# Seven weight clamps on VectorE instead of GpSimd, and the fifth tile's first products issued in the startup, in a fused attention and two-mixer kernel

## The chip, the cores and the metric

One core of one Trainium2 chip. The metric is the device time of one execution in microseconds; the median of three runs of the kernel before is 668.87 us (668.62 to 670.48).

## What is computed

Three stages follow each other on a batch of 4 sequences of 768 tokens; all numbers are float32.

```python
# 1. linear attention with a per-channel decay, 8 heads of 48
cur = einsum('bhd,bhe->bhde', u * kt, vt)
y[:, :, t] = einsum('bhd,bhde->bhe', rt, state + cur)
state = w * state + einsum('bhd,bhe->bhde', kt, vt)
# 2. a gated mixer, 384 -> 1024 -> 384
h = relu(x @ w_in)
conv_out = sum_k conv_w[k] * shifted(h, k)      # 3 taps over the tokens
x1 = (h * sigmoid(conv_out)) @ w_out
# 3. a normalised mixer, 384 -> 1536 -> 384
xn = (x1 - mean) / sqrt(var + 1e-6) * g_ln
out = x1 + relu(xn @ w_ch1) @ w_ch2
```

## The kernel before, in words

**Attention** works on 24 tiles of 128 tokens (n = 0 to 23), six to a sequence. `attn_tile(n)` is a generator. Its first part multiplies the tile's r and k by tables of decay powers (line 373, one VectorE instruction over both). Tiles 0 to 5 then take `light_tile`: z = r times k on VectorE (line 322), then at the next step dot products on TensorE, copies on ScalarE, a triangular select and a product on GpSimd (`affine_select`, line 335), then the products that make the output, and its split into a high and a low part. `decayed_k(n)` (line 252) multiplies the keys by their table. `startup()` (line 434) writes out by hand the order of tiles 0 to 3 and mixes in the first steps of the weight work. `attention()` (line 461) is a generator over the later tiles, from n = EARLY = 4 on; each `next` of it is one step.

**Weights** arrive in 22 pieces as pairs of 32-bit words (64-bit floats) and are converted on the chip. `wjob` (line 141) makes for each piece a load on SP's queue and a generator `steps()`: ScalarE takes the absolute value, `magnitude` (line 121) clamps it in place (line 125), VectorE shifts it and joins two more bit fields (`decode`, line 128), ScalarE writes the high part, and VectorE the low part (lines 168 and 170). `ahead()` (line 152) makes absolute value and clamp of the next piece at once after the last bit operation of a piece. The engine of the clamp is chosen there by the number of the piece, `me`: VectorE for pieces 0 to 9 (the first mixer's weights), GpSimd for pieces 10 to 21 (the second mixer's). `wdo(count)` (line 210) advances this work by so many steps. Pieces 15 to 21 are the second half of w_ch1 and the last four pieces of w_ch2.

**The first mixer** (`mixer1`, line 600) takes eight blocks of 384 tokens, and for each block eight rows of 128 channels: nine matmuls up, then ReLU on ScalarE, the convolution's centre tap on ScalarE (line 533) and its two other taps on VectorE (line 535), sigmoid, gate and a split into high and low part, and nine matmuls down, two or three rows later. After each row, `after1` (line 834) is called twice; it takes an attention step whenever `pace` has reached 5 (2.5 a call in the first two blocks, 2 later), and weight steps. In the first block that is `wdo(2)` at each call; from the second on one step at every fifth call.

**The second mixer** (`mixer2`, line 616) takes six blocks of 512 tokens with twelve rows of channels each. `after2` (line 860) advances the weight work by three steps after each row, until all pieces are made, which is within the first block. Between the blocks the next 512 tokens are fetched and normalised.

**Order.** Calls through `vo`, `ao`, `go`, `so` and `pe` keep the order of the program among themselves on their engine (VectorE, ScalarE, GpSimd, SP's queue, TensorE). All of TensorE's matmuls, the weight work and the early tiles are written this way. The other VectorE, ScalarE and GpSimd instructions (of the mixers, and most of the later tiles') are placed between them by a scheduler that simulates the program when it is built. Instructions made through these wrappers all show line 76 in the profile; the tile's name tells them apart: `wdec` is a weight piece in work, `rk` a tile's r and k, `kks` its decayed keys, `z` the product, `wih`, `wil`, `woh`, `wol`, `c1h`, `c1l`, `c2h`, `c2l` the high and low parts of the four weight matrices.

Of the kernel before, what the change touches and what calls it, by code (L numbers as in the profile page):

```python
# [49 lines left out]
def body(ctx, tc, r, k, v, w, u, w_in, conv_w, w_out, g_ln, w_ch1, w_ch2, rkT, krv, small, out):  # L50
# [28 lines left out]
    vo = InOrder(nc.vector)  # L79
    ao = InOrder(nc.scalar)  # L80
    so = InOrder(nc.sync)
    go = InOrder(nc.gpsimd)
# [35 lines left out]
    def words(st, n):  # L118
        return [st[:, 0:2 * n].rearrange("p (n two) -> p n two", two=2)[:, :, i] for i in range(2)]

    def magnitude(st, n, engine=go):

        t = ap.tile([128, WN], F32, tag="wd", name="wdec", bufs=2)[:, 0:n]
        ao.activation(out=t, in_=words(st, n)[1].bitcast(F32), func=AF.Abs)
        engine.tensor_scalar(out=t, in0=t, scalar1=W_MIN, scalar2=W_MAX, op0=ALU.max, op1=ALU.min)
        return t

    def decode(st, n, t):

        lo, hi = words(st, n)  # L130
        ti = t.bitcast(I32)
        vo.tensor_scalar(out=ti, in0=ti, scalar1=5, scalar2=2, op0=ALU.logical_shift_left,
                         op1=ALU.logical_shift_right)
        yield
        vo.scalar_tensor_tensor(out=ti, in0=lo, scalar=29, in1=ti, op0=ALU.logical_shift_right, op1=ALU.bitwise_or)
        yield
        vo.scalar_tensor_tensor(out=ti, in0=hi, scalar=-(2 ** 30), in1=ti, op0=ALU.bitwise_and, op1=ALU.bitwise_or)
# [3 lines left out]
    def wjob(src, n, hi, lo, scale=None):  # L141

        st, mag = [], []

        def load():
            st.append(io.tile([128, 2 * WN], I32, tag="st" if me >= 4 else "first", name="st", bufs=3 if me >= 4 else 4))
            dst = st[0][:, 0:2 * n]
            if len(src.shape) == 3:
                dst = dst.rearrange("p (a n) -> p a n", a=src.shape[1])
            so.dma_start(out=dst, in_=src.bitcast(I32))  # L150

        def ahead():
            if not mag:
                mag.append(magnitude(st[0], n, vo if me < 10 else go))

        def steps():
            ahead()
            t = mag[0]
            yield from decode(st[0], n, t)
            if me + 1 < min(len(wjobs), w_loaded[0]):  # L160
                wjobs[me + 1][2]()
            if len(src.shape) == 3:
                t = t.rearrange("p (a n) -> p a n", a=src.shape[1])
            kw = {} if scale is None else {"scale": gl[:, scale:scale + 1]}
            ao.activation(out=hi, in_=t, func=AF.Copy, **kw)
            yield
            if scale is None:
                vo.tensor_tensor(out=lo, in0=t, in1=hi.bitcast(F32), op=ALU.subtract)
            else:
                vo.scalar_tensor_tensor(out=lo, in0=t, scalar=kw["scale"], in1=hi.bitcast(F32),  # L170
                                        op0=ALU.mult, op1=ALU.subtract)
        me = len(wjobs)
        wjobs.append((load, steps(), ahead))
        return len(wjobs) - 1

# [28 lines left out]
    def wload(count):  # L204

        while w_loaded[0] < min(count, len(wjobs)):
            wjobs[w_loaded[0]][0]()
            w_loaded[0] += 1

    def wdo(count=1, last=None):  # L210

        for _ in range(count):
            while w_done[0] < (len(wjobs) if last is None else last + 1):
                wload(w_done[0] + 3)
                if next(wjobs[w_done[0]][1], "end") != "end":
                    break
                w_done[0] += 1
# [8 lines left out]
    def load_tile(n):  # L226
        if n >= NT:
            return
        own = "e" if n < EARLY else ""
        rk = io.tile([PR, 2, NP, C], F32, tag="rk" + own, name="rk", bufs=EARLY if own else 3)  # L230
        kt = io.tile([128, DM], F32, tag="k" + own, name="kt", bufs=EARLY if own else 2)
        rv = io.tile([128, DM + H * 64], F32, tag="rv" + own, name="rv", bufs=EARLY if own else 3)
        s_ = so
        s_.dma_start(out=rk.rearrange("x a p c -> x (a p c)"), in_=rkT[n])
        s_.dma_start(out=kt, in_=krv[n, :, 0:DM])
        if n >= EARLY:
            load_rows(n, s_, rv)
        loaded[n] = (rk, kt.rearrange("x (h d) -> x h d", h=H), rv[:, 0:DM].rearrange("x (h d) -> x h d", h=H),
                     rv[:, DM:].rearrange("x (h d) -> x h d", h=H), rv)
# [12 lines left out]
    def decayed_k(n):  # L252

        if n < LIGHT:
            vo.tensor_tensor(out=kks[:, n % 2, 0, :, 0:D], in0=loaded[n][1], in1=tku[:, 0], op=ALU.mult)
            return
        inputs(n).tensor_tensor(out=kks[:, n % 2, :, :, 0:D], in0=loaded[n][1].unsqueeze(1).to_broadcast([128, 2, H, D]), in1=tku,
                         op=ALU.mult)
# [45 lines left out]
    def inputs(n):  # L304
        return vo if n < HAND else nc.vector
# [102 lines left out]
    def state_sum(n):  # L408
        vt = loaded[n][3]
        if n % TPB != TPB - 1:  # L410
            pst = sums[n] = ps_a.tile([128, NP, D], F32, tag="pa", name="pst")
            for h in range(H):
                q0 = 64 * (h % 2)
                pe.matmul(pst[q0:q0 + 64, h // 2, :], lhsT=kks[:, n % 2, 0, h, :], rhs=vt[:, h, 0:D], start=True,
                          stop=True)

    def state_update(n):
        first, last = n % TPB == 0, n % TPB == TPB - 1
        v_, a_, g_ = ordered(n)
        if not last:  # L420
            pst = sums.pop(n)
            sn = ap.tile([PR, NP, D], F32, tag="sn", name="sn")
            if first:
                a_.activation(out=sn, in_=pst[0:PR], func=AF.Copy)
            else:
                v_.tensor_tensor(out=sn, in0=pst[0:PR], in1=state[0], op=ALU.add)
            if n % TPB < TPB - 2:
                state[0] = ap.tile([PR, NP, D], F32, tag="sw", name="sw")
                v_.tensor_tensor(out=state[0], in0=sn, in1=w128.to_broadcast([PR, NP, D]), op=ALU.mult)
            sb = sbd[(n + 1) % 2]  # L430
            a_.activation(out=sb[0:D, :, 0:D], in_=sn[0:D], func=AF.Copy)
            a_.activation(out=sb[64:PR, :, D:2 * D], in_=sn[64:PR], func=AF.Copy)

    def startup():

        tiles = {n: attn_tile(n) for n in range(EARLY + 1)}

        def on(n):
            next(tiles[n], None)

        decayed = decayed_k
        on(0), decayed(0), on(0)
        on(1), state_sum(0), state_update(0), decayed(1), on(1), state_sum(1)
        wdo(1)
        on(0), on(2), state_update(1), decayed(2)
        wdo(2)
        on(2), state_sum(2), on(0)
        wdo(1)
        on(1), on(3), state_update(2), decayed(3)
        wdo(2)  # L450
        on(3), state_sum(3), on(1)
        wdo(2)
        on(2), state_update(3)
        wdo(3)
        on(2), on(3)
        wdo(1)
        on(3)
        wdo(4)
        return tiles

    def attention(tiles):

        def go_on(n):
            if 0 <= n < NT:
                next(tiles.setdefault(n, attn_tile(n)), None)

        n = EARLY
        go_on(n)
        decayed_k(n)
        yield  # L470
        load_tile(n + 2)
        decayed_k(n + 1)
        go_on(n)
        yield
        for n in range(EARLY, NT):
            state_sum(n)
            state_update(n)
            go_on(n - 1)
            go_on(n + 1)
            yield  # L480
            go_on(n)
            go_on(n + 1)
            yield
# [333 lines left out]

    cst = tables()
    feed = attention(startup())
    for _ in conv_weights(cst):  # L820
        pass
# [120 lines left out]
```

## Time and profile before

| | us |
|---|---|
| median of three runs | 668.87 |
| the profiled execution | 670.22 |
| its span, first to last instruction | 668.4 |
| TensorE busy (matmuls) | 633.3 |
| VectorE busy | 437.4 |
| ScalarE busy | 261.9 |
| GpSimd busy | 122.5 |

Times in the trace are counted from the span's first instruction, in microseconds. A row of a timeline gives the start, the duration, the engine, the line, the operation, the tile written and the tiles read, the shape, and how many equal instructions in a row were merged; in brackets stands how long the engine had been idle before, and what ended that, as inferred from semaphores. PE is TensorE, DVE is VectorE, ACT is ScalarE, POOL is GpSimd and SPq is the queue on which SyncE issues loads and stores. Matmuls overlap, so TensorE's busy time counts only where it leaves gaps. The granted clock (PEclk) is a share of full speed.

### The profile page before, as it was taken

To read this page: it belongs to the slowest core of one execution; us is meant where nothing else is said; L and a number is where in the kernel's file an instruction comes from. 1 tells how busy PE (TensorE), PEld (TensorE's weight loads), DVE (VectorE), ACT (ScalarE), POOL (GpSimd) and SP (SyncE) were. 2 spreads that over 40 slices of the span, in tenths; PEclk is the share of its full clock that TensorE was granted. 3 is DMA by queue.
4 is the path that set the end of the run, shared out by engine and by line. 5 is a ranking of instruction groups with operands and counts; after the bars stand their busy time and mean duration, and the time that the engine had idled before them with its cause. 6 is when DMAs were issued, how large, how long until landed. Compare 5 with 4: busy or idle time off the path is not lost.

```text
span 668.4 us, 11712 instructions
## 1 busy us (share of the span) xinstructions
PE 633.3 (95%) x4803; PEld 573.2 (86%) x4803; DVE 437.4 (65%) x793; ACT 261.9 (39%) x514; POOL 122.5 (18%) x126
## 2 busy tenths in 40 slices
PE   9948898999998898999999999999999999999996
PEld 5747888989987897899998789999999899999995
DVE  7979999999999999878777953413422422422211
ACT  3455555465655655566764421211221111221110
POOL 6301621330332214112003620100100100100000
PEclk9876898999999999999999999999999999999999
DMA  8916434435262533102205302002001100200101
GB/s 268 313 49 209 144 106 151 135 100 185 71 215 68 173 114 115 37 1 84 71 13 177 95 0 89 8 0 86 10 0 48 49 0 29 67 0 7 42 0 52
DMA packets 25295, 56.51 MB, mean 85 GB/s; under 512 B 2961, under 2 KB 15378, under 8 KB 25234
## 3 DMA queue, kind: packets, MB, share of 16 engines
q1 hardware_dynamic: 25234, 55.68, 26.2%
q8 instruction: 40, 0.66, 0.4%
q14 instruction: 21, 0.17, 0.1%
HBM read 46.24 MB, written 9.44 MB: 83 GB/s over the span
## 4 chain that ended last, share of the span: by engine, by line
PE 50%; DVE 36%; ACT 4%; issue 4%; DMA 3%; POOL 1%; SPq 0%; DVEq 0%; ACTq 0%
PE acc L76 24%; PE psm L76 24%; DVE c L535 8%; DVE wdec L76 6%; DVE aT L389 3%; DVE c L516 3%; DVE gl L522 3%; DVE rk L373 2%; DMA x1b<-x_dram 1%; DVE rk L76 1%; DVE a L380 1%; DVE xl L398 1%; PE pxt L76 1%; DVE av L378 1%; DMA rk<-in_rkT_dram 1%
## 5 line engine op out<-in xcount | busy, mean ns | idle before, releaser
L549 DVE SCALAR_TENSOR_TENSOR rl<-psm,rh 128x512 fp32r<-128x512 f32 x72 | 49.6, 689 | 135.1 <-ACT rh L548 131.6
L548 ACT ACTIVATE rh<-psm 128x512 fp32r<-128x512 f32 x72 | 43.0, 597 | 196.1 <-PE psm L76 195.9
L76 PE MATMUL acc<-c2l,rh 128*128 128x384 f32 x288 | 97.2, 338 | 0.4 <-DVE c2l L76 0.4
L76 PE MATMUL acc<-c2h,rh 128*128 128x384 f32 x288 | 97.1, 337 | 0.0
L76 PE MATMUL acc<-c2h,rl 128*128 128x384 f32 x288 | 97.1, 337 | 0.0
L535 DVE SCALAR_TENSOR_TENSOR c<-h,tables,c 128x384 f32<-128x384 f32 x128 | 89.9, 704 | 7.0 <-ACT c L533 6.4
L76 PE MATMUL psm<-xnh,c1h 128*128 128x512 f32 x216 | 87.2, 404 | 0.8 <-ACT c1h L76 0.8
L76 PE MATMUL psm<-xnh,c1l 128*128 128x512 f32 x216 | 85.3, 395 | 0.3 <-DVE c1l L76 0.3
L76 PE MATMUL psm<-xnl,c1h 128*128 128x512 f32 x216 | 85.5, 396 | 0.0
L76 PE MATMUL psm<-xh,wih 128*128 128x386 f32 x192 | 71.3, 371 | 13.4 <-DVE xl L76 4.4
L76 PE MATMUL psm<-xl,wih 128*128 128x386 f32 x192 | 67.7, 353 | 0.0
L76 PE MATMUL psm<-xh,wil 128*128 128x386 f32 x192 | 67.7, 352 | 0.0
L76 PE MATMUL acc<-woh,gh 128*128 128x384 f32 x192 | 66.5, 347 | 0.0
L76 PE MATMUL acc<-woh,gl 128*128 128x384 f32 x192 | 65.0, 339 | 0.1
L76 PE MATMUL acc<-wol,gh 128*128 128x384 f32 x192 | 65.0, 339 | 0.0
L76 PEld LDWEIGHTS acc<-c2l,rh 128*128 128x128 f32 x288 | 54.1, 188 | 3.6 <-DVE c2l L76 0.8
L76 PEld LDWEIGHTS acc<-c2h,rh 128*128 128x128 f32 x288 | 54.1, 188 | 3.2
L76 POOL TENSOR_SCALAR wdec<-wdec 128x768 f32<-128x768 f32 (+1 forms) x13 | 40.1, 3085 | 86.4 <-ACT wdec L76 86.4
L76 PEld LDWEIGHTS acc<-c2h,rl 128*128 128x128 f32 x288 | 54.1, 188 | 0.0
L572 POOL TENSOR_TENSOR rs<-rs,nhalf 128x1 f32<-128x1 f32 x24 | 16.4, 691 | 199.4 <-DVE rs L571 198.9
L76 PEld LDWEIGHTS psm<-xh,wih 128*128 128x128 f32 x192 | 38.1, 199 | 17.0 <-ACT woh L76 4.6
L521 ACT ACTIVATE gh<-c 128x384 fp32r<-128x384 f32 x64 | 33.5, 523 | 47.2 <-DVE c L516 46.7
(133 smaller groups left out, 1142.3 us busy)
## 6 DMA issues: line engine op xcount, KB each, us to landing
rk<-in_rkT_dram SPq DMA_DIRECT2D x24, 448.0 KB, 4.4
st<-in_moe_w_ch_dram SPq DMA_DIRECT2D x12, 768.0 KB, 6.0
rv<-in_krv_dram SPq DMA_DIRECT2D x18, 448.0 KB, 4.8
kt<-in_krv_dram SPq DMA_DIRECT2D x24, 192.0 KB, 4.3
x_dram<-x SPq DMA_DIRECT2D x24, 192.0 KB, 2.1
x1b<-x_dram SPq DMA_DIRECT2D x24, 192.0 KB, 3.1
out_dram<-x1b SPq DMA_DIRECT2D x24, 192.0 KB, 1.9
st<-in_moe_w_in_dram SPq DMA_DIRECT2D x6, 512.0 KB, 9.2
```

What stands on the lines that cost most here:

```text
L76: return lambda *args, **kw: tc.keep_in_program_order(op(*args, **kw))
L373: inputs(n).tensor_tensor(out=rk, in0=rk, in1=trk, op=ALU.mult)
L378: v_.tensor_tensor(out=av, in0=kks[:, n % 2, 1, :, 0:D], in1=rt, op=ALU.mult)
L380: v_.tensor_reduce(out=a8.rearrange("x (q p) o -> x q (p o)", q=2), in_=av.rearrange("x (p q) d -> x q p d", q=2), axis=AX.X, op=ALU.add)
L389: v_.copy_predicated(out=aT[:, q], mask=later.bitcast(I32).unsqueeze(1).to_broadcast([128, NP, C]), data=dps[q])
L516: v_.tensor_tensor(out=st["c"], in0=st["h"][:, 1:T + 1], in1=st["c"], op=ALU.mult)
L521: a_.activation(out=st["gh"], in_=st["c"], func=AF.Copy)
L522: v_.tensor_tensor(out=st["gl"], in0=st["c"], in1=st["gh"].bitcast(F32), op=ALU.subtract)
L535: v_.scalar_tensor_tensor(out=c, in0=h[:, o:o + T], scalar=cw[:, tap, f:f + 1], in1=c, op0=ALU.mult, op1=ALU.add)
L548: a_.activation(out=gh[:, 0:cols], in_=ps[:, 0:cols], func=AF.Relu)
L549: v_.scalar_tensor_tensor(out=gl_[:, 0:cols], in0=ps[:, 0:cols], scalar=0.0, in1=gh[:, 0:cols].bitcast(F32), op0=ALU.max, op1=ALU.subtract)
L572: g_.tensor_tensor(out=rs[:, 1:2], in0=rs[:, 0:1], in1=nhalf, op=ALU.pow)
```

## The change

The clamp's engine becomes VectorE for pieces 15 to 21 as well, so GpSimd keeps those of pieces 10 to 14 (and the small one of the convolution's weights). In `startup()` the last four weight steps are split: after the first of them stand the first step of tile 4 (its r and k products and z) and its keys. In `attention()` the same two calls and the first `yield` are taken out.

```diff
--- before.py
+++ after.py
@@ -151,7 +151,7 @@
 
         def ahead():
             if not mag:
-                mag.append(magnitude(st[0], n, vo if me < 10 else go))
+                mag.append(magnitude(st[0], n, vo if me < 10 or me >= 15 else go))
 
         def steps():
             ahead()
@@ -455,7 +455,9 @@
         on(2), on(3)
         wdo(1)
         on(3)
-        wdo(4)
+        wdo(1)
+        on(4), decayed(4)
+        wdo(3)
         return tiles
 
     def attention(tiles):
@@ -465,9 +467,6 @@
                 next(tiles.setdefault(n, attn_tile(n)), None)
 
         n = EARLY
-        go_on(n)
-        decayed_k(n)
-        yield
         load_tile(n + 2)
         decayed_k(n + 1)
         go_on(n)
```

## Rows read from the trace of the kernel before

**Rows 1.** The page's chain that ended last: shares of the span by engine.

```profile
PE 50%; DVE 36%; ACT 4%; issue 4%; DMA 3%; POOL 1%; SPq 0%; DVEq 0%; ACTq 0%
```

**Rows 2.** Busy time by stage: stage and length, engines (instructions), PEclk, DMA share, GB/s.

```profile
52.50:60.00 7.50, 7.49 (x45) 6.84 (x45) 7.46 (x12) 3.40 (x7) 3.05 (x3) 0.50 0.43 138
52.50:130.00 77.50, 72.11 (x752) 66.08 (x753) 77.40 (x122) 42.09 (x85) 27.43 (x18) 0.90 0.50 156
130.00:280.00 150.00, 142.56 (x1550) 130.81 (x1549) 145.92 (x239) 84.04 (x176) 39.32 (x34) 1.00 0.38 122
346.00:396.00 50.00, 48.51 (x243) 42.51 (x242) 40.55 (x70) 21.35 (x34) 21.89 (x10) 1.00 0.29 91
396.00:655.00 259.00, 259.00 (x1318) 233.85 (x1317) 76.62 (x161) 44.35 (x77) 9.50 (x16) 1.00 0.09 28
```

**Rows 3.** Timeline of TensorE: start us, us, instruction [idle before <-releaser].

```profile
52.51 2.08 PE L76 MATMUL dps<-rk 48*128 48x128 f32 x16 [7.16 <-ACT wih L76]
```

**Rows 4.** Timeline of VectorE, 40 to 55 us.

```profile
40.99 1.42 DVE L76 SCALAR_TENSOR_TENSOR wdec<-st,wdec 128x512 int32<-128x512 int32 x2
...
44.01 0.69 DVE L76 TENSOR_TENSOR wil<-wdec,wih 128x512 fp32r<-128x512 f32 x1 [1.26 <-ACT wih L76]
...
46.88 1.27 DVE L535 SCALAR_TENSOR_TENSOR c<-h,tables,c 128x384 f32<-128x384 f32 x2 [0.68 <-ACT c L533]
...
51.19 1.22 DVE L76 TENSOR_TENSOR rk<-rk,tables 112x1024 f32<-112x1024 f32 x1
...
53.32 0.69 DVE L76 TENSOR_TENSOR z<-rk 112x512 f32<-112x512 f32 x1
53.92 0.55 DVE L76 TENSOR_TENSOR kks<-kt,tables 128x384 f32<-128x384 f32 x1
```

**Rows 5.** Timeline of ScalarE, 40 to 60 us.

```profile
42.97 0.49 ACT L532 ACTIVATE h<-psm 128x386 f32<-128x386 f32 x1 [1.63 <-PE psm L76]
43.35 0.62 ACT L76 ACTIVATE wih<-wdec 128x512 fp32r<-128x512 f32 x1
```

**Rows 6.** Timeline of SP's DMA queue.

```profile
42.47 15.17 SPq L76 DMA_DIRECT2D st<-in_moe_w_out_dram  x3
```

**Rows 7.** Timeline of GpSimd.

```profile
56.65 1.96 POOL L335 TENSOR_SCALAR_AFFINE_SELECT aT<-aT 128x512 f32<-128x512 f32 x2 [11.31 <-ACT aT L334]
...
294.07 3.29 POOL L76 TENSOR_SCALAR wdec<-wdec 128x768 f32<-128x768 f32 x1 [16.71 <-ACT wdec L76]
...
379.85 3.41 POOL L76 TENSOR_SCALAR wdec<-wdec 128x768 f32<-128x768 f32 x1 [2.81 <-ACT wdec L76]
```

**Rows 8.** The list of waits, 85 to 290 us: us in total, times, longest.

```profile
DVE c L535 <- ACT c L533: 1.5, 2, 1.0
```

**Rows 9.** Timeline of VectorE: a clamp of the startup, then 362 to 392 us.

```profile
34.66 0.56 DVE L76 TENSOR_SCALAR wdec<-wdec 128x768 f32<-128x768 f32 x1 [1.26 <-ACT wdec L76]
...
362.27 0.56 DVE L569 BATCH_NORM_STATS2 bs<-x1b 128x6 f32<-128x384 f32 x1 [3.85 <-DMA x1b<-x_dram]
...
368.71 1.10 DVE L76 SCALAR_TENSOR_TENSOR wdec<-st,wdec 128x768 int32<-128x768 int32 x1
...
372.19 1.02 DVE L76 SCALAR_TENSOR_TENSOR c1l<-wdec,smallt,c1h 128x768 fp32r<-128x768 f32 x1 [0.40 <-ACT c1h L76]
...
374.60 2.29 DVE L76 SCALAR_TENSOR_TENSOR wdec<-st,wdec 128x768 int32<-128x768 int32 x2
...
381.13 0.98 DVE L76 SCALAR_TENSOR_TENSOR wdec<-st,wdec 128x768 int32<-128x768 int32 x1
...
384.97 2.44 DVE L76 SCALAR_TENSOR_TENSOR wdec<-st,wdec 128x768 int32<-128x768 int32 x2
...
390.33 1.95 DVE L76 SCALAR_TENSOR_TENSOR wdec<-st,wdec 128x768 int32<-128x768 int32 x2
```

**Rows 10.** The list of TensorE's waits, 346 to 396 us.

```profile
PE psm L76 <- ACT c1h L76: 0.8, 1, 0.8
```

**Rows 11.** Timeline of ScalarE: the absolute value of a weight piece.

```profile
378.85 0.91 ACT L76 ACTIVATE wdec<-st 128x768 f32<-128x768 f32 x1 [0.65 <-DVE c2l L76]
```

## The prediction

> **What bounds the kernel now.** I read the chain of waits first, then a table of busy time by stage, then the single engines where the change acts. The chain that ends last is half TensorE and 36% VectorE [rows 1]: two regimes. The stage table shows where they part [rows 2]. From 52.5 to 130 us VectorE is busy 77.40 of 77.50 us while TensorE has 5.4 us idle: VectorE sets the pace. From 130 to 280 us they share it (VectorE idle 4.1 us, TensorE 7.4). From 346 to 396 us TensorE idles 1.5 us, and from 396 to 655 us not at all. So time can be won only in three places: VectorE's idle time before 52.5 us (saved there, it lets all that follows start earlier), waits of the two for each other from 130 to 280 us, and TensorE's 1.5 us at 346 to 396.
>
> One place stands out. TensorE does nothing for 7.16 us ahead of the dot products of the fifth tile (n = 4), which start at 52.51 us [rows 3]. The row names a copy on ScalarE; the operand that came last is that tile's product of r and k, which VectorE ran from 51.19 to 52.41 us [rows 4]. TensorE's order is written by hand, so the up-projection behind it waited too.
>
> **The change part by part. First, the fifth tile's products.** The calls that issue r, k times decay (1.22 us), z (0.69) and the keys (0.55) [rows 4] move from the first mixer's first step into the startup, between the fourth weight piece's low part and the fifth piece's middle operations. The work is the same 2.46 us; only idle time can be saved. In VectorE's order it now stands ahead of the two operations at 40.99 us, which ended at 42.41 and now end at 44.87 us. The ScalarE copy behind them ran from 43.35 to 43.97 us; it had stood behind ScalarE's first copy out of PSUM, which itself waited 1.63 us for TensorE [rows 5]. It now waits for its own operand alone: 44.9 to 45.5 us. VectorE's next low part started at 44.01 after 1.26 us of waiting [rows 4]; it now starts at 45.5, so 1.5 us later with 2.46 us more work done. **Gain 1.0 us.** The convolution's weights and the first channel row's taps come behind it: the taps at 46.88 move to about 48.4, and the wait of 0.68 us ahead of them [rows 4] stays, a round trip to ScalarE. Bounds: nothing (the 1.26 us stays, the work has only moved) to 1.9 us (both waits fill). I take 1.0 because that wait has a named cause that goes.
>
> With its first yield gone, the attention's generator is one step further at every slot of the mixer. What the second step issues moves with it: dot products on TensorE (now behind the first up-projection), ScalarE's copies, GpSimd's selects, the next keys on VectorE, and three loads of the seventh tile on SP's queue. That queue issued three weight loads from 42.47 to 57.64 us ahead of them [rows 6]; now fewer stand ahead, and since the loads need buffers that are free, or free after the keys at about 43.5 us, what stands behind them waits for nothing new: cost nothing. GpSimd's queue was empty for 11.31 us before the first of its selects [rows 7]: nothing either.
>
> TensorE's gap of 7.16 us closes. Most of that is not time won, for VectorE is full until 130 us, and TensorE must stop for it later instead. What the lead can return is VectorE waiting, through ScalarE, on a late TensorE. From 85 to 290 us those are 1.5 us in two waits, the longer 1.0 [rows 8]. I take the longer, **1.0 us**; the bounds are 0 and the 4.1 us that VectorE idles from 130 to 280 us.
>
> TensorE's granted clock is 0.50 from 52.5 to 60 us, behind the idle stretch, the lower of its two levels (1.2 of 2.4 GHz) [rows 2]. Without the gap it may rise sooner. VectorE being the bound there, I put that at nothing; without this cover it is part of the faster rival.
>
> **Second, the clamps.** Seven clamps leave GpSimd, where one takes 3.3 to 3.4 us [rows 7], for VectorE, where the same shape took 0.56 us [rows 9]: 3.9 us more VectorE work. GpSimd's time was hidden: VectorE's waits there name ScalarE and a load, not GpSimd [rows 9]. The first clamp of the seven, at 294 us, falls where TensorE is full: nothing. The six others lie between 349 and 389 us. Each now stands between a piece's last bit operation and its low part, where VectorE waited for ScalarE's high part, as for 0.40 us at 372.19 [rows 9], so about four of six are covered. Two are not: VectorE resumed at 362.27 us after 3.85 us of waiting for a load [rows 9], and from there to 378.9 us it stood on the chain, up to TensorE's longest wait of that stage, 0.8 us [rows 10]. Two clamps there cost 1.1 us. Against that, two-input VectorE operations ran long beside GpSimd's clamps: the pairs at 374.60 and 384.97 us took 2.29 and 2.44 us, a pair at 390.33 us, with GpSimd idle, 1.95; a single one took 1.10 at 368.71 against half of 1.95 [rows 9]. The first (0.35) and the last (0.15) lie on the chain. Net: **1.1 - 0.5 = 0.6 us lost**. Bounds: 1.5 us won (all of TensorE's idle time there goes) and 3.4 us lost (six clamps, nothing covered).
>
> Beside those rows stands a rule. The Trainium skill, "SBUF — State Buffer", section "Who interferes with whom", has VectorE and GpSimd share a port pair as an exclusive lock. The trace agrees only in part: the operation at 381.13 us ran wholly beside a GpSimd clamp (379.85 to 383.26) in 0.98 us [rows 7, 9]. Were every excess (1.0 us with the pair at 384.97) given back on the chain, as a strict lock would have it, the total would be 667.0, inside the forecast's own range.
>
> **Sum**: -1.0 - 1.0 + 0.6 = -1.4 us. The profiled execution took 670.22 us (668.4 of span, 1.8 around it), so the same conditions give 668.8; it stands 1.35 us above the median of 668.87, against which I forecast **667.5 us**. What a measurement can tell from no change is 0.3%, 2.0 us: below 666.9 is faster, above 670.9 slower.
>
> **The rivals.** *Nothing moves* (0.20): the convolution's weights become what the start waits for, ScalarE's order is built anew and the wait at 44 us reappears behind it; lead and loss cancel: 668.9. For it: the waits there hang on ScalarE, not on VectorE's load.
>
> *The lead is worth more* (0.23): TensorE's head start, at the full clock sooner, removes half of VectorE's 4.1 us idle (2.0 instead of 1.0), and a free GpSimd removes half of TensorE's 1.5 us late (0.8 won instead of 0.6 lost): 668.87 - 1.0 - 2.0 - 0.8 = 665.1. For it: from 130 us the two engines are even, so any lead counts; against it: until 130 us VectorE has no idle time in which a lead could be kept.
>
> *A clamp that waits* (0.12, the slower side): VectorE runs in order, and the clamp needs ScalarE's absolute value. In the startup, where VectorE makes the clamps, such a wait cost 1.26 us [rows 9]. Behind it then stand the piece's low part, the next shift and the low halves of the activations, for which TensorE's down-projections wait. If the three clamps from 357 to 377 us each wait 1.26 us and lie bare (0.56), the price is 5.5 us in place of 0.6: 668.87 - 2.0 + 5.5 = 672.4. It decides where the absolute value ends later than the previous piece's last bit operation; before, one ended at 379.76 us, 1.4 us ahead of that operation's start at 381.13 [rows 9, 11]. The Trainium skill, "Perfetto Trace Analysis", section "Optimizing Scalar/DVE Operations", points the same way: with VectorE saturated, offloading to ScalarE or even GpSimd may make sense. Here VectorE idles 9.4 of the 50 us from 346 us on [rows 2], which speaks against it.
>
> **How the numbers follow.** The forecast has 0.45, its own range 666.2 to 669.0. A third of that (0.14) lies below 666.9; with the larger lead, faster has 0.37. Slower is the waiting clamp and a small tail: 0.13. The same: 0.50. The range runs from 664.7 (most of the larger lead) to 670.4 (bare clamps and no gain at the start), leaving out some 0.2.
>
> **What would show it.** Right: the fifth tile's product of r and k near 41 us; no idle over 2 us on TensorE from 45 to 52 us; VectorE's wait at 44 us down to about 0.3 us, the first taps about 1.5 us later; VectorE still full to 130 us; TensorE's idle time at 346 to 396 us between 1 and 2.5 us. Wrong: VectorE idle by 1 us or more ahead of a clamp, TensorE's gap turning up whole elsewhere, or TensorE's idle time after 346 us changed by over 1 us.

## The result and the profile after

The changed kernel takes 674.48 us (median of 4 runs, 673.55 to 676.16), beside 669.23 us for the kernel before on the same chip (668.62 to 670.48). The ratio is 1.0079 [1.0053 to 1.0105]: 5.3 us slower. The forecast was 667.5 us, in a range from 664.7 to 670.4; the sign is wrong and the time lies outside the range. Its profiled execution took 674.12 us with a span of 672.4 us, against 670.22 and 668.4 before. Line numbers of the changed kernel are one lower below line 470.

Start where the chain was read before: the page's chain that ended last, of the kernel after.

```profile
PE 61%; DVE 26%; ACT 4%; DMA 4%; issue 3%; POOL 0%; DVEq 0%; ACTq 0%; SPq 0%
```

VectorE's share fell from 36% to 26% and TensorE's rose from 50% to 61% [rows 1], with no work for TensorE added. The table of busy time by stage, after, with the columns of [rows 2], says where:

```profile
52.50:130.00 77.50, 59.76 (x681) 54.05 (x673) 71.60 (x115) 38.24 (x78) 17.02 (x14) 0.89 0.47 142
130.00:280.00 150.00, 141.13 (x1512) 129.52 (x1511) 145.71 (x237) 83.71 (x173) 38.10 (x35) 0.98 0.37 118
346.00:396.00 50.00, 49.98 (x258) 45.13 (x258) 45.03 (x83) 24.92 (x41) 3.52 (x4) 1.00 0.28 91
```

Two things moved, in opposite directions. From 346 to 396 us TensorE is busy 49.98 us where it was busy 48.51 [rows 2]: its idle time there is gone. But from 52.5 to 130 us, where VectorE had been busy 77.40 of 77.50 us, it is now busy 71.60, and TensorE 59.76 against 72.11. So both engines stand idle in the stretch that had been VectorE's alone. Cut finer, the same view from 40 to 100 us, first of the kernel before (the whole stretch in the last line):

```profile
40.00:52.50 12.50, 5.36 (x18) 5.05 (x18) 9.51 (x20) 7.05 (x12) 0.29 (x1) 0.64 0.25 69
52.50:70.00 17.50, 16.58 (x153) 15.03 (x153) 17.43 (x28) 9.92 (x19) 3.05 (x3) 0.74 0.59 196
70.00:85.00 15.00, 13.59 (x125) 12.89 (x126) 15.00 (x20) 8.93 (x17) 12.60 (x5) 0.89 0.66 188
85.00:100.00 15.00, 13.75 (x137) 12.43 (x137) 14.96 (x25) 7.87 (x17) 3.36 (x3) 1.00 0.31 91
sum 60.00, PE 49.28 PEld 45.41 DVE 56.91 ACT 33.77 POOL 19.31; mean PE 12.32 PEld 11.35 DVE 14.23 ACT 8.44 POOL 4.83
```

and of the kernel after:

```profile
40.00:52.50 12.50, 11.86 (x81) 10.38 (x83) 9.61 (x20) 6.88 (x14) 2.29 (x4) 0.60 0.50 154
52.50:70.00 17.50, 13.96 (x178) 12.20 (x169) 17.50 (x30) 12.96 (x27) 3.82 (x3) 1.00 0.38 115
70.00:85.00 15.00, 1.48 (x14) 1.48 (x16) 14.33 (x20) 4.35 (x6) 6.53 (x3) 0.51 0.71 225
85.00:100.00 15.00, 14.94 (x137) 13.53 (x137) 10.30 (x16) 6.31 (x15) 0.49 (x3) 0.92 0.26 76
sum 60.00, PE 42.24 PEld 37.60 DVE 51.74 ACT 30.50 POOL 13.14; mean PE 10.56 PEld 9.40 DVE 12.94 ACT 7.63 POOL 3.28
```

The gap that the change closed is the first line: TensorE's busy time from 40 to 52.5 us rose from 5.36 to 11.86. It came back in the third: 1.48 of 15 us busy, at half the granted clock (0.51, the lower of the two levels, 1.2 GHz). VectorE is still nearly full there (14.33), and then, from 85 to 100 us, has nothing to do for 4.70 us, where it had idled 0.04. Summed over 60 us, VectorE gets through 5.17 us less work and TensorE through 7.04 less.

The single rows follow. TensorE's timeline after, the dot products of the fifth, sixth and seventh tile (n = 4, 5, 6); the first answers to [rows 3]:

```profile
42.65 2.08 PE L76 MATMUL dps<-rk 48*128 48x128 f32 x16 [0.64 <-ACT h L531]
...
54.61 1.16 PE L76 MATMUL dps<-rk 48*128 48x128 f32 x16
...
83.52 2.08 PE L76 MATMUL dps<-rk 48*128 48x128 f32 x16 [15.29 <-DVE rk L76]
```

The wait of 7.16 us is 0.64 us, and two tiles later stands one of 15.29 us, for the r and k product of tile 6. VectorE's timeline after, with what answers to [rows 4] first:

```profile
39.94 1.22 DVE L76 TENSOR_TENSOR rk<-rk,tables 112x1024 f32<-112x1024 f32 x1
...
44.38 0.69 DVE L76 TENSOR_TENSOR wil<-wdec,wih 128x512 fp32r<-128x512 f32 x1 [0.36 <-ACT wih L76]
...
47.01 0.80 DVE L76 TENSOR_SCALAR wdec<-wdec 128x24 int32<-128x24 int32 x1 [1.60 <-POOL wdec L76]
...
49.14 1.27 DVE L534 SCALAR_TENSOR_TENSOR c<-h,tables,c 128x384 f32<-128x384 f32 x2 [0.69 <-ACT c L532]
...
72.00 0.95 DVE L76 TENSOR_TENSOR kks<-kt,tables 128x768 f32<-128x768 f32 x1
...
75.54 0.56 DVE L378 TENSOR_TENSOR av<-kks,rv 128x384 f32<-128x384 f32 x1
...
78.28 0.55 DVE L380 TENSOR_REDUCE a<-av 128x8 f32<-128x384 f32 x1
78.75 1.36 DVE L76 SCALAR_TENSOR_TENSOR wdec<-st,wdec 128x768 int32<-128x768 int32 x1
80.03 0.54 DVE L380 TENSOR_REDUCE a<-av 128x8 f32<-128x384 f32 x1
80.49 0.94 DVE L76 SCALAR_TENSOR_TENSOR wdec<-st,wdec 128x768 int32<-128x768 int32 x1
81.36 2.11 DVE L76 TENSOR_TENSOR rk<-rk,tables 112x1024 f32<-112x1024 f32 x1
83.39 0.95 DVE L76 TENSOR_TENSOR wol<-wdec,woh 128x768 fp32r<-128x768 f32 x1
85.70 1.34 DVE L389 COPY_PREDICATED aT<-tables,dps 128x512 f32<-128x512 int32 x2 [1.36 <-PE dps L76]
90.02 1.23 DVE L373 TENSOR_TENSOR rk<-rk,tables 112x1024 f32<-112x1024 f32 x1 [2.98 <-DMA rk<-in_rkT_dram]
```

Tile 6's product stands at 81.36, between the last bit operation of the tenth weight piece (80.49) and its low part (83.39). Its operand was there long before: SP's queue after issued that load at 44.24 us, and the load for which VectorE waits at 90.02 only when tile 6's dot products were through.

```profile
44.24 0.39 SPq L76 DMA_DIRECT2D rk<-in_rkT_dram  x1
...
85.67 0.33 SPq L76 DMA_DIRECT2D rk<-in_rkT_dram  x1
```

GpSimd's timeline after shows the clamp of the convolution's weights, which VectorE awaits at 47.01, behind the selects of tile 4. The program issues that clamp first; the selects (line 335) don't go through `go`, and it is the scheduler that placed them ahead. Some 0.6 of the 1.60 us is ScalarE's, whose absolute value for the clamp ended at 46.02 us, behind tile 4's copies:

```profile
45.49 1.23 POOL L335 TENSOR_SCALAR_AFFINE_SELECT aT<-aT 128x512 f32<-128x512 f32 x2 [12.99 <-ACT aT L334]
46.68 0.29 POOL L76 TENSOR_SCALAR wdec<-wdec 128x24 f32<-128x24 f32 x1
```

A measure of progress that no single wait can distort is the start of each row of the first mixer, taken from TensorE's timeline (a row begins with the first of its nine up-projection matmuls; us):

| row | before | after | clamps alone (below) |
|---|---|---|---|
| 1st | 39.7 | 38.8 | 40.8 |
| 5th | 71.4 | 61.4 | 72.5 |
| 6th | 76.4 | 85.5 | 78.2 |
| 10th | 98.3 | 107.0 | 99.3 |
| 64th, the last | 342.7 | 349.3 | 344.0 |

After is 10.0 us ahead at the fifth row, 9.1 behind at the sixth and 6.6 behind at the last. The whole loss is made at one place. (Of the 10.0 us, 0.9 are there at the first row already. The runs below with the same startup begin it anywhere from 38.8 to 41.0 us, so a difference of one or two us between two profiles need not come from an edit.)

### The profile page after: what moved, and what is told of

Its sections match the earlier page's. It is cut to its first block, busy times and chain, and to the rows that moved or that the text cites. A ratio compares the mean times of both kernels' runs of the same rounds, so it can differ in the third digit from the quotient of the medians.

```text
span 672.4 us, 11693 instructions
## 1 busy us (share of the span) xinstructions
PE 629.1 (94%) x4803; PEld 570.2 (85%) x4803; DVE 440.1 (65%) x800; ACT 261.5 (39%) x514; POOL 91.5 (14%) x119
## 4 chain that ended last, share of the span: by engine, by line
PE 61%; DVE 26%; ACT 4%; DMA 4%; issue 3%; POOL 0%; DVEq 0%; ACTq 0%; SPq 0%
PE psm L76 29%; PE acc L76 28%; DVE c L534 6%; DVE wdec L76 4%; DMA rk<-in_rkT_dram 3%; DVE aT L389 2%; DVE c L515 2%; DVE rk L373 2%; DVE gl L521 2%; DVE rk L76 1%; PE pxt L76 1%; PE dps L76 1%; DVE a L380 1%; ACT c L514 1%; DVE av L378 1%
## 5 line engine op out<-in xcount | busy, mean ns | idle before, releaser
L534 DVE SCALAR_TENSOR_TENSOR c<-h,tables,c 128x384 f32<-128x384 f32 x128 | 88.1, 692 | 6.4 <-ACT c L532 5.4
L514 ACT ACTIVATE c<-c 128x384 f32<-128x384 f32 x64 | 33.5, 524 | 48.7 <-DVE c L534 48.3
L76 PE MATMUL dps<-rk 48*128 48x128 f32 x384 | 30.5, 297 | 20.3 <-DVE rk L76 17.4
L76 PEld LDWEIGHTS psm<-xnh,c1l 128*128 128x128 f32 x216 | 40.6, 188 | 10.0
```

The source lines that it names most:

```text
L76: return lambda *args, **kw: tc.keep_in_program_order(op(*args, **kw))
L514: a_.activation(out=st["c"], in_=st["c"], func=AF.Sigmoid)
L534: v_.scalar_tensor_tensor(out=c, in0=h[:, o:o + T], scalar=cw[:, tap, f:f + 1], in1=c, op0=ALU.mult, op1=ALU.add)
```

## The experiments

Ratios are to the kernel before on the same chip, with 95% intervals; edits are to the kernel named. At the end stands one table of them all.

### The two halves apart

Before, with the clamps' line alone:

```diff
-                mag.append(magnitude(st[0], n, vo if me < 10 else go))
+                mag.append(magnitude(st[0], n, vo if me < 10 or me >= 15 else go))
```

> The clamps of pieces 15 to 21 alone move to VectorE; startup and attention are as before. Theory A (the loss of the whole change comes from the start: the r and k product of tile 6 is tied behind the last bit operation of weight piece 9, and TensorE waits 15.3 us for it): no loss here, and since TensorE's idle time at 346 to 396 us fell from 1.5 us to nothing in the changed kernel, 1 to 1.5 us are won: about 668.0. Theory B (the clamps load VectorE where it is on the chain): 3 to 5 us lost, 672 to 674.

Measured: 666.97 us, 0.9966 [0.9946 to 0.9986]: 2.3 us faster, and faster than both kernels. Busy time from 346 to 396 us, the counterpart of [rows 2]:

```profile
346.00:396.00 50.00, 49.91 (x256) 44.85 (x255) 42.48 (x77) 23.55 (x37) 3.50 (x4) 1.00 0.29 91
```

TensorE's idle time went from 1.49 to 0.09 us, though VectorE does 1.93 us more. The clamps are a gain.

The change with the clamps left on GpSimd:

```diff
-                mag.append(magnitude(st[0], n, vo if me < 10 or me >= 15 else go))
+                mag.append(magnitude(st[0], n, vo if me < 10 else go))
```

> The startup's part alone: tile 4's products in the startup and the attention one step ahead; the clamps stay on GpSimd. Theory A: the whole loss and none of the clamps' gain, 5 to 7 us over before, about 675.5, with the wait of some 15 us on TensorE before the dot products of tile 6. Theory B: no loss, 667 to 669.

Measured: 675.85 us, 1.0098 [1.0067 to 1.0128], with the same wait in TensorE's timeline:

```profile
85.26 2.08 PE L76 MATMUL dps<-rk 48*128 48x128 f32 x16 [15.32 <-DVE rk L76]
```

So the move costs 6.6 us by itself, and the clamps take back 1.3 of it (0.0019; their gain alone was 0.0034), though the intervals of the two runs overlap, so the 1.3 is not clear of noise. The stage table of this run agrees that there is less to take back:

```profile
346.00:396.00 50.00, 49.47 (x259) 44.87 (x258) 42.23 (x77) 25.27 (x43) 20.73 (x10) 1.00 0.29 91
```

With the clamps still on GpSimd, TensorE idles 0.53 us there and not 1.49. So of the 1.47 us that went in the change, the clamps account for about 0.5; why the move alone takes the rest was not tested.

### The move taken apart: earlier products, or the lead

The changed kernel with the empty step of `attention()` put back, so that only the products are earlier:

```diff
         n = EARLY
+        yield
         load_tile(n + 2)
```

> The whole change, but the attention's generator keeps an empty first step, so its steps stand at the slots where they stood before and only the products of tile 4 have moved. Theory A: the tie of tile 6's product to weight piece 9 is gone, TensorE never waits over 8 us after 40 us, and the time is that of before less what both parts win: 666 to 668.5. Theory C (the products in the startup themselves make the loss, since the convolution's weights and all behind them come later): 672 to 675.

Measured: 671.17 us, 1.0023 [1.0003 to 1.0044]. The time lies between the two forecasts: the wait of 15 us is gone, but TensorE waits for tile 6's masked copy, as its timeline has it:

```profile
90.55 0.69 PE L76 MATMUL psm<-xh,wih 128*128 128x386 f32 x1 [7.92 <-DVE aT L389]
```

VectorE idles 3.43 us from 85 to 100. So the earlier products alone cost 3.8 us over the clamps alone (0.0057), where the prediction had them win 1.0.

The clamps alone and the lead, with the products left in `attention()`:

```diff
         decayed_k(n)
-        yield
         load_tile(n + 2)
```

> The kernel before with the seven clamps on VectorE, and of the change's start only the lead: the empty step ahead of the loop of attention is gone, but the fifth tile's products stay where they were. Theory A (the lead is what costs: tile 6's chain stands behind the weight pieces whatever the products do): TensorE has a wait of 8 to 15 us ahead of tile 6's dps or yps, VectorE idles 3 to 5 us more than before between 85 and 100, 671 to 674. Theory B (the moved products are what costs, since 3 to 4 us went with them alone in the run with the step kept): 666 to 668.5, and VectorE as full as before. Between 669 and 671 each has a share.

Measured: 673.98 us, 1.0056 [1.0038 to 1.0075], as the theory of the lead had it in its time: 6.0 us (0.0090) for the lead alone. The place of the waits is other than expected: TensorE's timeline has 9.07 us ahead of the fifth tile, whose products are now too late for the lead, and 4.42 for tile 6; and VectorE idles 0.20 us from 85 to 100, but 1.92 from 70 to 85, for GpSimd's product behind the selects of tile 5, which took 8.27 us in this run (see the last section). How much of the 6.0 is due to that was not separated.

```profile
53.31 2.08 PE L76 MATMUL dps<-rk 48*128 48x128 f32 x16 [9.07 <-ACT wih L76]
...
83.36 2.08 PE L76 MATMUL dps<-rk 48*128 48x128 f32 x16 [4.42 <-issue]
```

Each half of the move costs, and the two together cost 7.6 us (0.0113), less than their sum of 9.8. In each there is a stop of TensorE at tile 6 (7.92 us for its masked copy, 4.42 ahead of its dot products).

### Three waits taken away one by one

First the tie. Tile 6's product is made through `vo`, which keeps it behind whatever `vo` made just before it; with the lead that is the tenth piece's last bit operation. Freed for this tile:

```diff
-        inputs(n).tensor_tensor(out=rk, in0=rk, in1=trk, op=ALU.mult)
+        (nc.vector if n == 6 else inputs(n)).tensor_tensor(out=rk, in0=rk, in1=trk, op=ALU.mult)
```

> The whole change, but tile 6's product of r and k is issued without the call that keeps the program's order, so that the scheduler may place it ahead of the weight work. Theory A: TensorE's wait of 15.3 us ahead of tile 6's dot products falls below 3 us, and the time to 666 to 669.5. Theory C, or the one step of lead being the loss through later loads: 672 to 675, with the waits for loads of r and k from 85 to 205 us as in the changed kernel.

Measured: 673.83 us, 1.0058 [1.0035 to 1.0081], at most 1.4 us (0.0021) better than the change and within the rival's range. VectorE's timeline has the product 29 us earlier than in the change, and tile 6's masked copy 6.2 us later:

```profile
52.24 1.23 DVE L373 TENSOR_TENSOR rk<-rk,tables 112x1024 f32<-112x1024 f32 x1 [1.86 <-DMA rk<-in_rkT_dram]
...
91.88 1.33 DVE L389 COPY_PREDICATED aT<-tables,dps 128x512 f32<-128x512 int32 x2
```

TensorE's timeline of the same run shows where the wait went, to the tile's last products:

```profile
92.66 2.53 PE L76 MATMUL yps<-aT,rv 128*32 128x128 f32 x32 [9.15 <-DVE aT L389]
```

Second, the load for which VectorE waits 2.98 us at 90.02. It is that of tile 9's product, which the scheduler had put ahead of tiles 7 and 8; with one more tile made through `vo` it stands where it is written:

```diff
-HAND = 9
+HAND = 10
```

> The changed kernel with HAND = 10, so that the ninth index's r and k product is placed behind what was traced before it and no longer stands ahead of the seventh's and eighth's on VectorE. Theory A (VectorE's dry spell is what costs, and its largest piece is the wait of 2.98 us for that product's load): the wait goes, VectorE's idle time between 85 and 100 falls from 4.7 to about 2, and the time to 671 to 672. Rival (the spell is set by TensorE's late dps of tile 6; something else waits in its place): 673.5 to 675.

Measured: 676.25 us, 1.0106 [1.0076 to 1.0135]: the rival held, with a time above its range. VectorE idles 5.48 us from 85 to 100 and waits as long at the same place, now for the first tap of the sixth row, which TensorE began only at 86.2 us:

```profile
86.38 1.34 DVE L389 COPY_PREDICATED aT<-tables,dps 128x512 f32<-128x512 int32 x2 [1.36 <-PE dps L76]
90.61 1.27 DVE L534 SCALAR_TENSOR_TENSOR c<-h,tables,c 128x384 f32<-128x384 f32 x2 [2.89 <-ACT c L532]
```

Third, the convolution's clamp, freed from the selects:

```diff
-        t = magnitude(cst, 3 * NF1)
+        t = magnitude(cst, 3 * NF1, vo)
```

> The changed kernel with the clamp of the convolution weights on VectorE in place of GpSimd, so that it no longer stands behind the fourth tile's selects. Theory A (the wait of 1.60 us at 47 is lost for good): the wait goes, one clamp of about 0.5 us is added, and the time falls by about 1, to 673 to 673.8. Rival (what VectorE wins at 47 it spends idle between 85 and 100, where it runs out of work): no change, 674 to 675, with VectorE's idle time in that stretch above 5.

Measured: 676.98 us, 1.0112 [1.0082 to 1.0142]: the rival held again, with a time above its range and VectorE idle for 5.23 us from 85 to 100. The wait of 1.60 us at 47 is now one of 0.63 at 46.10, for ScalarE's absolute value, and tile 6's dot products start at 83.52 us, to the hundredth as in the changed kernel (TensorE waits 16.22 us for them here). What is won at 47 us is lost at 85.

### The order of the weight pieces against tile 6

What no run so far set out to change is what stands ahead of tile 6's keys and sums on VectorE: the keys, their product with r (`av`), the sums (`a`) and the masked copy come in between the steps of the weight pieces, and `wdo(2)` after each half row hands those out as fast as before the change. The changed kernel with half that rate for the first ten calls (`slot` counts the calls of `after1`, two a row; the expectations of this group say rows for them):

```diff
-                wdo(2, wo_job[NF1 - 1])
+                wdo(2 if slot[0] > 10 else 1, wo_job[NF1 - 1])
```

> The changed kernel with one step of the weight pieces a row instead of two for the first ten rows, so that tile 6's products, keys and sums stand ahead of the last two or three pieces on VectorE. Theory A (tile 6 stands behind the pieces, and that makes TensorE's wait of 15 us and VectorE's dry spell): TensorE's longest wait between 60 and 100 falls under 8 us, VectorE idles 1 to 3 us there instead of 5, 668 to 671. Rival (the order of the pieces doesn't matter, since TensorE's rows need them as soon): the wait moves to a row that needs a piece, and the time stays at 673 to 676.

Measured: 669.59 us, 0.9998 [0.9980 to 1.0016], 5.4 us (0.0081) less than the change with the same lead, the same products and the same clamps. VectorE's timeline has tile 6's product at 67.52 us and its masked copy at 73.35, against 81.36 and 85.70 in the change:

```profile
67.52 1.21 DVE L76 TENSOR_TENSOR rk<-rk,tables 112x1024 f32<-112x1024 f32 x1
...
73.35 1.32 DVE L389 COPY_PREDICATED aT<-tables,dps 128x512 f32<-128x512 int32 x2
```

and VectorE no longer runs dry from 85 to 100 us (busy 15.00 of 15). A stop remains, two tiles on; TensorE's timeline:

```profile
101.21 2.08 PE L76 MATMUL dps<-rk 48*128 48x128 f32 x16 [5.12 <-issue]
```

The same rate for six calls, and an uneven one with a pause of three calls:

```diff
-                wdo(2, wo_job[NF1 - 1])
+                wdo(2 if slot[0] > 6 else 1, wo_job[NF1 - 1])
```

> As the run with slower weight pieces, but one step a row for six rows instead of ten; tile 6's keys and sums still stand ahead of the last three pieces. Theory A (only the order of tile 6 against the pieces matters; the stall of row 9 came from pieces that then were late): the stall of 13 us between rows 9 and 10 shrinks, 667 to 669. Rival (the lead makes TensorE wait for VectorE's backlog at one tile or another whatever the order): some row between 5 and 10 takes over 9 us again, 669 to 673.

```diff
-                wdo(2, wo_job[NF1 - 1])
+                wdo(1 if slot[0] < 3 else 2 if slot[0] > 5 else 0, wo_job[NF1 - 1])
```

> The changed kernel with the weight pieces at one step a row for two rows, none for three and two from then on: tile 6's keys stand eight places further ahead, and its sums ahead of piece 7 too. Theory A: no wait over 6 us on TensorE ahead of tile 6, VectorE idle no more than 7 us from 40 to 280, 666 to 668.5. Rival (the pieces are needed by row 9 anyway, and come later here): a wait of some 10 us there, 669 to 672.

Measured: 670.12 us, 1.0002 [0.9986 to 1.0018], and 673.67 us, 1.0062 [1.0040 to 1.0085]. Six calls do as well as ten; the stall after them is shorter (the tenth row starts 10.9 us after the ninth, with ten calls 14.2), but above the 9 us of the rival, and the time lies in the rival's range. The pause was a miss, with a time above both forecasts: it starved the row that needed the next piece (TensorE waited 3.69 us at 68.54 us for that piece's high part), and VectorE waited 2.61 us at 78.67 us for another piece's high part and idled 3.43 us from 60 to 85. The order matters in both directions.

Without the lead and with the slower pieces (products early, as in the first run of the second group):

```diff
         n = EARLY
+        yield
         load_tile(n + 2)
...
-                wdo(2, wo_job[NF1 - 1])
+                wdo(2 if slot[0] > 10 else 1, wo_job[NF1 - 1])
```

> The changed kernel without the lead (the empty step is kept) and with one step of the weight pieces a row for ten rows. Without the slower pieces it was 671.2, with waits of 1.0 and 1.2 us on VectorE for the sixth index's and ninth index's loads and 7.9 us on TensorE for a mask. Theory A (tile 6 behind the pieces is what costs there too): VectorE's idle time from 40 to 280 falls from 11.2 to 7 or 8, 667 to 669. Rival (the loads of weights that stand ahead of the tiles' loads on SP are what costs there): no change, 670.5 to 672.

Measured: 668.73 us, 0.9982 [0.9962 to 1.0003], inside the forecast time, 2.7 us (0.0041) below the same kernel with fast pieces. So the slower pieces help without the lead too. The interval overlaps that of the clamps alone: the earlier products and the slower pieces together win nothing over them. What the slower pieces would do for the clamps alone no run shows, so the cost that is left of the earlier products is not known by itself. VectorE's idle time from 40 to 280 us fell less than expected, from 11.2 to 9.5, all of it and more between 85 and 100 us.

### The price of VectorE's time

Idle time may be only a sign. So the clamps alone, with needless work for VectorE in the first block (after the tenth call of `after1`):

```diff
+                if slot[0] == 10:
+                    dm = sp.tile([128, 512], F32, tag="dm", name="dm", bufs=1)
+                    vo.memset(dm, 0.0)
+                    for _ in range(8):
+                        vo.tensor_tensor(out=dm, in0=dm, in1=dm, op=ALU.mult)
```

> The kernel before with the seven clamps on VectorE, and after the tenth row of the first mixer one memset and eight needless products of 128x512 on VectorE, in program order: by the 0.69 us of the 128x512 split about 5.5 us, with the memset 5.9. It prices VectorE's time in the first mixer by itself. Theory A (VectorE is the bound there, so time lost on it there is lost at the end): the time rises by 5 to 6.5 over the clamps alone (667.0), to 672 to 673.5. Rival (rows wait for TensorE and loads anyway, so that VectorE's idle time is an outcome and not the cause): under 2 us more, 667 to 669.

Measured: 671.61 us, 1.0024 [1.0006 to 1.0042], 3.9 us (0.0058) above the clamps alone. The groups of VectorE's instructions on that tile (min/median/max in ns, then first and last start):

```profile
L76 DVE TENSOR_TENSOR dm<-dm x8: 671/678/686, 85.8 to 113.4; 128x512 f32<-128x512 f32 x8
L76 DVE MEMSET dm<- x1: 485/485/485, 83.7 to 83.7; 128x512 f32 x1
```

Eight times 0.678 and 0.485 are 5.9 us of work, and 3.9 of them, two thirds, arrive at the end. Neither forecast had that: VectorE sets the pace there for the most part. The size is loose: the intervals of the two runs leave some 2 to 5.7 us, an estimate that takes them as independent, so that "wholly" is not ruled out.

### All runs side by side

| run | ratio | VectorE busy, 40 to 100 us | tile 6's last products begin, us |
|---|---|---|---|
| clamps alone | 0.9966 | 56.90 | 93.1 |
| slower pieces, no lead | 0.9982 | 57.75 | 85.5 |
| slower pieces, ten calls | 0.9998 | 57.84 | 82.8 |
| before | 1 | 56.91 | 92.0 |
| slower pieces, six calls | 1.0002 | 57.27 | 80.7 |
| products early, no lead | 1.0023 | 53.74 | 95.9 |
| lead alone | 1.0056 | 54.10 | 94.7 |
| tile 6 untied | 1.0058 | 53.41 | 92.7 |
| pieces with a pause | 1.0062 | 53.78 | 85.9 |
| the change | 1.0079 | 51.74 | 93.9 |
| the move, clamps on GpSimd | 1.0098 | 51.56 | 96.0 |
| HAND = 10 | 1.0106 | 51.76 | 95.1 |
| convolution's clamp on VectorE | 1.0112 | 51.62 | 93.9 |

The third column sorts the runs in three groups, and the ratio follows them (the run with needless work is left out, as that counts as busy). The fourth fits the reason: as long as the pieces run at their old rate, tile 6's last products begin between 92 and 96 us, whatever TensorE's order. The lead brings TensorE to tile 6 earlier, but not tile 6 to TensorE. An early tile 6 is not enough, as the run with a pause shows (85.9 us, and 1.0062).

## Why the prediction was wrong

**The start** went nearly as written in its rows, but the gain of 1.0 us did not come. Tile 4's product ran at 39.94 us ("near 41"; this execution begins the first row 0.9 us earlier than the one before), TensorE has no idle time over 2 us from 45 to 52, and the wait at 44 us fell from 1.26 to 0.36 ("about 0.3"); the taps came 2.3 us later ("about 1.5"), their wait stayed (0.69). What failed in these rows is "GpSimd's queue was empty for 11.31 us before the first of its selects [rows 7]: nothing either". With the lead, those selects start at 45.49 instead of 56.65 us and stand ahead of the convolution's clamp, and VectorE waits 1.60 us at 47.01. So VectorE's busy time from 40 to 52.5 us rose by 0.10 us and not by 1.0. That wait is no cause of the slower time, though: cut to 0.63 us, it left the time no lower. What the term had wrong is what follows an earlier TensorE: with the earlier products and no lead 3.8 us were lost where 1.0 was to be won, by the same stop for tile 6.

**The stop** is the step that failed, and the lead makes it longest. The prediction said of the gap of 7.16 us that "TensorE must stop for it later instead", and priced that stop at nothing because "VectorE is full until 130 us". The stop came, at twice the length: 15.29 us, and VectorE idled 4.70 us from 85 to 100. It was full only as long as it had a backlog. TensorE's matmuls keep the program's order (`pe`): moved one step ahead, tile 6's dot products stand ahead of the sixth row, while VectorE still delivers tile 6 among the last of its ten weight pieces. During the stop TensorE feeds no row; VectorE uses up its pieces and tile work, and at 85 us has neither a row nor a load to go on with. The list of what moves with the step named dot products, copies, selects, keys and loads, but not the place of tile 6's own instructions among the pieces on VectorE, which decides the most of it.

The slower pieces show it: with that order alone altered, 5.4 of the 7.6 us between the change and the clamps alone came back. Half of that, 2.7 us, they give without the lead as well; the lead costs 3.7 us (0.0056) with the fast pieces and the early products, and 1.1 (0.0016, within the intervals) with the slower ones. How the remaining 2.2 divide among the early products, the later stop at 101 us and the interval of the measurement was not separated. Nor does VectorE's lost work explain all by its price: 5.2 us at two thirds are 3.4 of the 7.6; the rest has no measured cause.

**The clamps** had the wrong sign as a sum: forecast 0.6 lost, measured 2.3 won alone (interval 0.9 to 3.6). The bound of 1.5, "all of TensorE's idle time there goes", was the right value: the clamps taken as bare were made in time that had been idle. VectorE's wait for the load of [rows 9], 3.85 us, is down to 1.40 in its timeline after (1.79 with the clamps alone, 2.45 with the move alone, so not all of that is the clamps'):

```profile
366.02 0.56 DVE L568 BATCH_NORM_STATS2 bs<-x1b 128x6 f32<-128x384 f32 x1 [1.40 <-DMA x1b<-x_dram]
```

No VectorE wait over 1 us stands ahead of a clamp, so the rival of a waiting clamp did not come; the slower side came by way of the stop, which the prediction named as a sign of error ("TensorE's gap turning up whole elsewhere") and gave no chance. Of the lock between VectorE and GpSimd, the trace after gives both answers again: with GpSimd free, the two operations that took 2.29 us as a pair [rows 9] run singly in 0.95 each, and the pair that took 2.44 takes 1.94, as VectorE's timeline shows,

```profile
378.17 0.95 DVE L76 SCALAR_TENSOR_TENSOR wdec<-st,wdec 128x768 int32<-128x768 int32 x1
...
380.00 0.95 DVE L76 SCALAR_TENSOR_TENSOR wdec<-st,wdec 128x768 int32<-128x768 int32 x1
...
389.33 1.94 DVE L76 SCALAR_TENSOR_TENSOR wdec<-st,wdec 128x768 int32<-128x768 int32 x2
```

and beside the selects of tiles 6 and 7, on GpSimd after,

```profile
81.19 4.09 POOL L383 TENSOR_SCALAR_AFFINE_SELECT aT<-a 128x1024 f32<-128x1024 f32 x2
```

the product at 81.36 took 2.11 us where it takes 1.22 elsewhere, while the low part at 83.39, within them too, took its usual 0.95. The Trainium skill, "SBUF — State Buffer", section "Who interferes with whom", has a VectorE instruction with two inputs in SBUF contend for a locked port pair with a GpSimd instruction that reads SBUF: the product at 81.36 agrees, the low part at 83.39 does not show it. The Trainium skill, "Perfetto Trace Analysis", section "Optimizing Scalar/DVE Operations", warns that offloading between VectorE and GpSimd might not help because they share that port; the clamps alone fit, since taking them back from GpSimd won 2.3 us with VectorE the busier for it. That the port is the reason is not shown: one clamp also takes 2.8 to 3.5 us on GpSimd before and 0.55 on VectorE after.

## What to carry to other kernels

Before a consumer is moved earlier on an engine that runs in order, find when its producer delivers, and what stands ahead of the producer on its own engine: everything behind the moved consumer waits for that date. "The other engine is full anyway" holds only while it has work that doesn't depend on the one being stopped; ask what feeds it during the stop. And measure parts of a change apart: here one half alone wins 2.3 us and the other alone loses 6.6.

## What was not expected of the hardware

The same two selects of 128x512 on GpSimd differ more than the row of before let one think (1.96 us [rows 7]): 1.23 us at 45.49 us after the change, 6.37 in the kernel before for the next tile, and 8.27 in the run with the lead alone, by GpSimd's timelines of these two:

```profile
71.43 6.37 POOL L335 TENSOR_SCALAR_AFFINE_SELECT aT<-aT 128x512 f32<-128x512 f32 x2 [11.73 <-ACT aT L334]
...
68.68 8.27 POOL L335 TENSOR_SCALAR_AFFINE_SELECT aT<-aT 128x512 f32<-128x512 f32 x2 [8.45 <-ACT aT L334]
```

In the latter run VectorE worked beside them without a pause up to 75.9 us and then waited 1.92 us for GpSimd's next product. Spans of GpSimd in a profile are rough, and no run tested the cause, so a forecast should not take a GpSimd row from one place for another.
